# A transformer block on one core: one of four query weight sums made anew on VectorE, output products that advance two token tiles together, and smaller changes to what is loaded when

## Chip, core and metric

The kernel runs on one NeuronCore of one Trainium2 chip. The metric is the device time of one execution in microseconds (us), lower is better. The time before is the median of seven executions. In addition one execution was recorded by the hardware profiler; all stage times below are from that record.

## What is computed

One conditioned transformer block on 2048 tokens of width 1024, in bf16 (the reference, cut to what matters):

```
mod = silu(c) @ w_mod            # six rows of 1024: sa, ca, ga, sb, cb, gb
h = layernorm(x) * (1 + ca) + sa
q = h @ wq                       # 32 query heads of 128 -> wq is 1024 x 4096
k, v = last 512 rows of the caches, 4 kv heads, each used by 8 query heads
o = softmax(q k^T / sqrt(128)) v # per head, 2048 x 512 scores
x = x + ga * (o @ wo)            # wo is 4096 x 1024
h = layernorm(x) * (1 + cb) + sb
x = x + gb * ((silu(h @ w_gate) * (h @ w_up)) @ w_down)    # 3584 wide
```

## The kernel before

**Fast products.** The query projection (except for the first eight heads), the output projection (except in the first chunk) and the feed-forward part are done by a Strassen-Winograd scheme: a 2 x 2 block product takes seven block products in place of eight. It needs four sums of weight blocks and four sums of input blocks. `PRO` and `product` give the seven products: A11 B11, A12 B21, four of a sum S by a sum T (number 0 to 3 in the lists), one of S4 by B22, and one of A22 by the last T.

**Stages.** The tokens are worked in four chunks of 512. In chunk 0 (to about 197 us in the profile) attention runs over 32 heads, and the output projection is a plain one (`oproj_plain`). Chunks 1 to 3 each have 32 heads of attention (about 197 to 310, 360 to 468, 517 to 629 us) and then `oproj` (to about 360, 517 and 675 us). The feed-forward part follows, in two stretches of 1024 tokens.

**One iteration of attention.** The loop variable `i` counts heads over all chunks (`NA` = 128), `h` is the head within the chunk. In an iteration TensorE does, in this order: a part of the query projection for heads four ahead (`q_first` or `q_third`), the scores of head `i + 1`, another part (`q_second` or `q_fourth`), and the product with the values (`pv`) of head `i`. VectorE drains the query products (L636, L640, L674) and normalises the attention output (reciprocal L707, product L708). ScalarE does the exponentials (L691). The engines are in order; the tracker `T.op` sets the semaphore waits from the buffers that an instruction reads and writes.

**Query weights and their sums.** Four heads share one group of weights. Per group and chunk, `load_wq` (L301) loads the weights, into one of two slots. The four sums T of a group are formed on VectorE once, in chunk 0 (`weight_sums`, L579), into a slot of `tq`, and stored to a DRAM tensor `wq_sums` (`store_sums`, L590), 1024 KB per group. Chunks 1 to 3 load all four back (`load_sums`, L596). The load for the group two ahead is emitted at `i % 4 == 0`, and waits until TensorE has done the last product of the group two before it, since there are two slots. The sum with number 1 is used first in a group, by product 6 in `q_second`; sum 1 is b22 minus sum 0.

**The SP queue.** SyncE (SP) issues in order, and one queue carries in attention: the weight loads, the sums, the loads of `x` (L389 for the next layer norm, L275 for the residual, four per chunk at h = 8, 12, 16, 20), the columns of `w_mod` (L902), the transposes of each head's output (`oturn`, L714) and of the normalised input (`ln_turn`, L372), both by DMA, and ten of the output projection's weight units (`load_unit`, L806).

**The output projection's units.** Weights come in 28 units of 512 KB per chunk, four per product of `PRO`, in ten slots. In chunks 1 to 3 the first ten are loaded by SP at h = 5, 7, ... 23. Within `oproj` each of two token tiles (`k`) runs through a whole product before the other. A slot is free after the second tile is through it, so `load_unit(ch, u + NUN, 1)`, issued by ScalarE's queue, is emitted at 5/8, 6/8, 7/8 and 8/8 of each product. The partial results are copied from PSUM by ScalarE (L862, L864) or added into the residual on VectorE (`take_product`, L884 to L888).

**Second layer norm, and the sums of w_down.** `ln2[1]` normalises the second half of the first feed-forward stretch; it starts at h = 14 of chunk 3, and whatever is not done is finished at h = 29. `wd_sums` forms four sums of `w_down` in a single buffer `t_` during the first stretch, and stores them (L1331) with one DMA of 512 KB per row block, after the fourth sum.

Of the kernel before, what the change touches and what calls it, by code (L numbers as in the profile page):

```python
# [3 lines left out]
ALU = mybir.AluOpType  # L4
# [38 lines left out]
class _Tracker:  # L43
    def __init__(self):
        self.synced = {}

    def op(self, st, emit, reads=(), writes=(), after=()):


        req = {}  # L50

        def need(s, c):
            if req.get(s, 0) < c:
                req[s] = c

        for b in reads:
            if b.last_write is not None:
                need(*b.last_write)
        for b in list(writes) + list(after):
            if b.last_write is not None:  # L60
                need(*b.last_write)
            for s, c in b.reads.items():
                need(s, c)
        if st.dma and st.count:
            need(st, st.count)
        done = self.synced.setdefault(id(st.issuer), {})
        for s, c in req.items():
            if s is st and st.self_exempt:
                continue
            if done.get(s, 0) >= c:  # L70
                continue
            st.issuer.wait_ge(s.sem, c)
            done[s] = c
        ins = emit()
        st.count += st.inc
        ins.then_inc(st.sem, st.inc)
        for b in reads:
            b.reads[st] = st.count
        for b in writes:
            b.last_write = (st, st.count)  # L80
            b.reads = {}
# [37 lines left out]
def bass_adaLN_cond__sliding_block_cached__swiglu_ffn__prompt_kernel(  # L119
# [140 lines left out]
    with nc.Block() as block:  # L260

        @block.gpsimd
        def _(g):
# [281 lines left out]
            B_tq = [bufs("tq%d_" % i, 4) for i in range(NWQ)]  # L545
            tq = [M.take((AT_TQ + 8 * i) * KB, [4, 4, 256], F16, B_tq[i]) for i in range(NWQ)]
            Q_tq = [dq("q_tq%d" % i) for i in range(NWQ)]
            Q_ts = dq("q_ts")
            wq_t = nc.dram_tensor("wq_sums", (HG * 2, P, 4096), F16).ap()
            B_wqt = bufs("wqt", HG * 2)  # L550
# [30 lines left out]
            def weight_sums(g, st, e, which):  # L581
                sl = g % NWQ
                w_, t_, bt = wq_sb[sl], tq[sl], B_tq[sl]
                b11, b12, b21, b22 = w_[:, 0:4, 0:256], w_[:, 0:4, 256:512], w_[:, 4:8, 0:256], w_[:, 4:8, 256:512]
                for k in which:
                    x, y, extra = ((b12, b11, []), (b22, t_[:, 0], [bt[0]]), (b22, b12, []), (b21, t_[:, 1], [bt[1]]))[k]
                    tt_(st, e, t_[:, k], bt[k], x, y, ALU.subtract, B_wq[sl] + extra)

            def store_sums(g):
                T.op(Q_ts, lambda: SP.dma_start(wq_t[g % HG], tq[g % NWQ].rearrange("p a b c -> p (a b c)")),  # L590
                     reads=B_tq[g % NWQ], writes=[B_wqt[g % HG]])

            def load_sums(g):
                if g >= NCH * HG:
                    return
                T.op(Q_tq[g % NWQ], lambda: SP.dma_start(tq[g % NWQ].rearrange("p a b c -> p (a b c)"), wq_t[g % HG]),  # L596
                     reads=[B_wqt[g % HG]], writes=B_tq[g % NWQ])

# [8 lines left out]
            def product(p0, m):  # L607
# [8 lines left out]
                for kc in range(4):  # L616
                    if t_i is not None:
                        lhsT, lb = tq[sl][:, t_i, kc, w_lo:w_lo + P], B_tq[sl][t_i]
                    elif m == 1:
# [162 lines left out]

            PRO = (("A11", "B11"), ("A12", "B21"), ("S2", 1), ("S1", 0), ("S3", 2), ("S4", "B22"), ("A22", 3))
            NPO = Hq // 2
# [5 lines left out]

            def load_unit(ch, u, st=0):

# [12 lines left out]
                e = (SP, A)[st]  # L805
                T.op(Q_un[st][sl], lambda: e.dma_start(dst, src), reads=rd, writes=[B_un[sl]])  # L806

            def o_first(ch, k, p):
# [3 lines left out]
                   [B_oT[2 * p][0], B_un[sl]], PB[(QBK, XBK)[k]], loose=True)  # L812

            def oproj(ch, done_first, each):
                ab, cb = [QBK, XBK], [OBK, OBK + 1]
                B_e1, B_u1, B_u2 = bufs("e1_", NPO // 4), bufs("u1_", 2), bufs("u2_", 2)
# [21 lines left out]
                sums(3)  # L838
                for n, (a_, _) in enumerate(PRO):
                    for k in range(2):  # L840
                        b = (ab, cb)[n in (1, 4, 6)][k]
                        for p in range(NPO):
                            if n == 0:
                                if (k, p) not in done_first:
                                    o_first(ch, k, p)
                            else:
                                lo, hi = slice(k * P, (k + 1) * P), slice(256 + k * P, 256 + (k + 1) * P)
                                lhsT, lb = {
                                    "A12": (oT[:, 2 * p + 1, lo], B_oT[2 * p + 1][0]), "A22": (oT[:, 2 * p + 1, hi], B_oT[2 * p + 1][1]),
                                    "S1": (e1[:, p, lo], B_e1[p // 4]), "S2": (oT_s[:, 2 * p, lo], B_oT[2 * p][0]),  # L850
                                    "S3": (oT_s[:, 2 * p, hi], B_oT[2 * p][1]), "S4": (oT_s[:, 2 * p + 1, lo], B_oT[2 * p + 1][0])}[a_]
                                u = n * (NPO // NPU) + p // NPU
                                sl = (ch * UPC + u) % NUN
                                mm(bank(b), lhsT, unit[sl][:, p % NPU, :], p == 0 and n in (1, 4), p == NPO - 1, [lb, B_un[sl]],
                                   PB[b], loose=True)
                            if p % NPU == NPU - 1:
                                u = n * (NPO // NPU) + p // NPU
                                if k == 1 and u + NUN < UPC:
                                    load_unit(ch, u + NUN, 1)
                                each()  # L860
                        if n in (0, 3):
                            T.op(ACT, lambda: A.activation(u1[k], bank(b), AF.Copy), writes=PB[b] + [B_u1[k]])  # L862
                        elif n == 2:
                            T.op(ACT, lambda: A.activation(u2[k], bank(b), AF.Copy), writes=PB[b] + [B_u2[k]])  # L864
                        else:
                            half, hf = {1: (0, 0), 4: (1, 1), 5: (0, 1), 6: (1, 0)}[n]
                            u_ = None if n == 5 else (u2[k], B_u2[k]) if n == 6 else (u1[k], B_u1[k])
                            take_product(b, u_, x_sb[:, 2 * half + k, :], BX[2 * half + k], ga_bc, B_ga[hf], hf, k)
                            if n >= 5:
                                keep_rows(ch * TPC + 2 * half + k)  # L870
                    if n == 0:
# [130 lines left out]
            for i in range(NA):  # L1002
                ch, h = divmod(i, Hq)
                p0 = i - i % 2 + LEAD
                if ch == 0 and h in (13, 17, 22):
                    load_wo((13, 17, 22).index(h))
                if ch and h % 2 and 5 <= h < 5 + 2 * NUN:
                    load_unit(ch, h // 2 - 2)
                if ch and h in (8, 12, 16, 20):
                    load_x(ch * TPC + h // 4 - 2)  # L1010
                at_xl = [AT_XL + 2 * j for j in range(3)]
# [4 lines left out]
                if ch == NCH - 1 and h == 3:  # L1016
                    ln2[0] = ln_task(range(TPC), True, at_xl, (AT_N, AT_N + 2), scale=(g2, B_g2, sb, B_sb))
                    tasks.append(ln2[0])
                if ch == NCH - 1 and h == 14:
                    finish(mod_rest)  # L1020
# [26 lines left out]
                if p0 >= PLAIN:  # L1047
                    if i % 2 == 0:
                        q_second(p0)
                    else:  # L1050
                        q_fourth(p0)
                exps(i + 1, 2)
                if h == Hq - 5 and ch + 1 < NCH:
                    input_sums((ch + 1) % 2, (0, 1))
# [17 lines left out]
                g = i // 4 + 2  # L1072
                if i % 4 == 0 and i >= 8 and g - 2 * 0 >= HG + 2:
                    load_sums(g)
# [231 lines left out]
            wd_t = nc.dram_tensor("wd_sums", (4, P, NPR * 512), F16).ap()  # L1306
            B_wdt = bufs("wdt", NPR)
            Q_ds, Q_dk = [dq("q_ds%d" % i) for i in range(2)], dq("q_dk")

            def wd_sums():  # L1310
# [13 lines left out]
                for r in range(NPR):  # L1324
                    w_ = dr[r % 2]
                    b11, b12, b21, b22 = w_[:, 0, 0:512], w_[:, 0, 512:D], w_[:, 1, 0:512], w_[:, 1, 512:D]
                    for k in range(4):
                        x, y, extra = ((b12, b11, []), (b22, t_[:, 0], [B_ds[0]]), (b22, b12, []), (b21, t_[:, 1], [B_ds[1]]))[k]
                        tt_(DVE, V, t_[:, k], B_ds[k], x, y, ALU.subtract, [B_dr[r % 2]] + extra)
                        yield  # L1330
                    T.op(Q_dk, lambda: SP.dma_start(wd_t[:, :, r * 512:(r + 1) * 512].rearrange("k p n -> p k n"), t_),  # L1331
                         reads=B_ds, writes=[B_wdt[r]])
                    load(r + 2)
# [10 lines left out]
            def load_wd(n):  # L1344
# [6 lines left out]
                for j in range(2):  # L1351
                    if isinstance(which, int):
                        src = wd_t[which][:, j * hp * CH:(j + 1) * hp * CH]
                        dst = wd[i][:, j * hp:(j + 1) * hp, :].rearrange("p a b -> p (a b)")
                        rd = B_wdt
                    else:
# [110 lines left out]
```

## Time and profile before

| | |
|---|---|
| time, median of 7 | 1185.4 us (1184.01 to 1188.8) |
| profiled execution | 1187.78 us; its span 1186.0 us |
| granted TensorE clock, mean | 0.996 |
| TensorE (PE) busy | 1155.0 us, 97% |
| VectorE (DVE) busy | 809.3 us, 68% |
| ScalarE (ACT) busy | 498.1 us, 42% |
| DMA moved | 253.42 MB, 214 GB/s on average |
| chain that ended last | PE 89%, DMA 6%, DVE 3% |
| load of a group's four sums | 1024 KB, 22 times, 7.2 us to landing |
| `x` load | 256 KB, 28 times, 6.1 us to landing |

The rows are shares over the whole span, and stages differ: in attention DVE is busy for up to 90% of some stretches, in the output projection much less. "PE busy" is time in which the profile has a matmul in flight; the number of matmuls in a stretch tells whether they come at full pace. The DMA share in windows is a sum over packets, and it can exceed 1[...].

### The profile page before, as it was taken

Reading aid. Unit: us, or ns where it says so; the run is one execution under the profiler, and the core shown is the slowest. Engines: PE = TensorE matmul, PEld = TensorE weight load, DVE = VectorE, ACT = ScalarE, POOL = GpSimd, SP = SyncE. Lnnn points to the kernel's source line nnn. Section 1 sums busy time; section 2 is a strip of 40 time slices with the busy share of each in tenths; the row PEclk is TensorE's granted clock in tenths of the full one; section 3 lists DMA queues with packets and bytes.
Section 4 is the critical chain, followed back from the end, with each engine's and each line's share of the span. In section 5 each row is a group of like instructions: output and inputs, shape, how many; then the busy total and the mean of one; then the engine's idle time right before and its main releaser. Section 6 shows DMA issues by size and latency. Waiting matters only on the chain.

```text
span 1186.0 us, 20701 instructions
## 1 busy us (share of the span) xinstructions
PE 1155.0 (97%) x7838; PEld 665.7 (56%) x7838; DVE 809.3 (68%) x1792; ACT 498.1 (42%) x736; POOL 20.3 (2%) x41
## 2 busy tenths in 40 slices
PE   6999999999999999999899999999999999999998
PEld 4677645777647777468674444444444444444443
DVE  4888737876728877457677588888457777776214
ACT  4676502666306765147561144444210344444110
POOL 1000000000000000000000000000010000000000
PEclk9999999999999999999999999999999999999999
DMA  9999796999769997959979766564896232321733
GB/s 304 234 269 260 209 357 220 304 283 288 214 234 251 296 302 182 305 143 274 266 179 284 239 197 194 164 200 138 272 285 191 72 106 73 96 83 62 249 133 133
DMA packets 282627, 253.42 MB, mean 214 GB/s; under 512 B 109728, under 2 KB 244896, under 8 KB 278688
## 3 DMA queue, kind: packets, MB, share of 16 engines
q1 hardware_dynamic: 252656, 189.70, 59.7%
q10 hardware_dynamic: 29872, 62.40, 15.2%
q8 instruction: 62, 1.02, 0.4%
q14 instruction: 37, 0.30, 0.1%
HBM read 195.04 MB, written 32.51 MB: 192 GB/s over the span
## 4 chain that ended last, share of the span: by engine, by line
PE 89%; DMA 6%; DVE 3%; SPq 1%; issue 1%; ACT 0%; POOL 0%; DVEq 0%
PE ps L265 89%; DMA arena<-wq_sums 3%; DMA arena<-arena 1%; DMA arena<-in_w_mod_dram 1%; SPq L284 1%; DMA wd_sums<-arena 1%; DVE arena L708 1%; DVE arena L1187 0%; DVE arena L579 0%; DVE arena L412 0%; DVE arena L640 0%; ACT arena L932 0%; DVE arena L674 0%; DVE arena L707 0%; DVE arena L376 0%
## 5 line engine op out<-in xcount | busy, mean ns | idle before, releaser
L265 PE MATMUL ps<-arena 128*128 128x512 bf16 (+5 forms) x7789 | 1151.6, 310 | 22.8 <-DMA arena<-wq_sums 8.2
L265 PEld LDWEIGHTS ps<-arena 128*128 128x128 bf16 (+1 forms) x7789 | 662.4, 98 | 511.2 <-issue 12.8
L691 ACT ACTIVATE arena<-ps 128x1024 bf16<-128x1024 f32 x256 | 249.8, 1022 | 39.3 <-PE ps L265 36.4
L579 DVE TENSOR_TENSOR arena<-arena 128x512 f16<-128x512 bf16 (+2 forms) x488 | 208.4, 471 | 25.4 <-DMA wo_sums<-arena 11.5
L634 ACT ACTIVATE arena<-ps 128x256 f32<-128x256 f32 x134 | 51.3, 383 | 195.2 <-PE ps L265 194.4
L1175 DVE TENSOR_TENSOR arena<-ps,arena 128x512 f16<-128x512 f32 x112 | 77.2, 689 | 39.4 <-PE ps L265 37.3
L1168 ACT ACTIVATE arena<-ps 128x512 f32<-128x512 f32 x112 | 66.9, 597 | 73.6 <-PE ps L265 73.6
L708 DVE TENSOR_TENSOR arena<-ps,arena 128x512 bf16<-128x512 f32 x128 | 88.5, 692 | 4.9 <-DVE arena L707 0.5
L1197 ACT ACTIVATE ps<-ps 128x512 f32<-128x512 f32 x56 | 32.6, 582 | 127.1 <-PE ps L265 126.9
L640 DVE TENSOR_TENSOR arena<-ps,arena 128x256 bf16<-128x256 f32 x180 | 75.6, 420 | 12.0 <-PE ps L265 8.2
L884 DVE TENSOR_TENSOR arena<-ps,arena 128x512 f32<-128x512 f32 x34 | 23.4, 690 | 84.2 <-PE ps L265 84.1
L1187 DVE TENSOR_TENSOR arena<-ps,arena 128x512 bf16<-128x512 f32 x56 | 38.5, 688 | 29.3 <-ACT arena L1182 29.3
L707 DVE RECIPROCAL arena<-ps 128x4 f32<-128x4 f32 x128 | 23.1, 181 | 40.6 <-PE ps L265 39.6
L887 DVE TENSOR_TENSOR arena<-ps,arena 128x512 bf16<-128x512 f32 x22 | 15.2, 689 | 46.4 <-PE ps L265 46.4
L1182 ACT ACTIVATE arena<-ps 128x512 f16<-128x512 f32 x56 | 33.3, 594 | 31.6 <-PE ps L265 31.6
L412 DVE BATCH_NORM_STATS2 arena<-arena 128x6 f32<-128x512 bf16 x56 | 38.5, 687 | 6.4 <-DMA arena<-x_mid 6.2
L915 DVE SCALAR_TENSOR_TENSOR arena<-arena 128x512 f32<-128x512 bf16 x56 | 41.6, 743 | 0.1
L1182 ACT ACTIVATE arena<-arena 128x512 f16<-128x512 f16 x56 | 34.8, 622 | 4.9 <-DVE arena L1175 4.9
L835 DVE TENSOR_TENSOR arena<-arena 128x1024 f16<-128x1024 bf16 (+1 forms) x48 | 29.7, 685 | 7.2 <-DMA arena<-arena 7.2
L636 DVE COPY arena<-ps 128x256 f32<-128x256 f32 x46 | 19.4, 421 | 20.1 <-PE ps L265 19.8
L363 POOL TENSOR_TENSOR arena<-arena 128x1 f32<-128x1 f32 x30 | 17.8, 592 | 872.8 <-DVE arena L361 870.0
L674 DVE CAST arena<-ps 128x256 bf16<-128x256 f32 x60 | 25.2, 420 | 8.4 <-PE ps L265 7.0
(61 smaller groups left out, 208.7 us busy)
## 6 DMA issues: line engine op xcount, KB each, us to landing
arena<-wq_sums SPq DMA_DIRECT2D x22, 1024.0 KB, 7.2
arena<-in_A_wq_dram SPq DMA_DIRECT2D x42, 512.0 KB, 5.1
arena<-wo_sums ACTq DMA_DIRECT2D x42, 512.0 KB, 6.4
arena<-in_B_w_gate_dram SPq DMA_DIRECT2D x28, 512.0 KB, 4.2
arena<-in_B_w_up_dram SPq DMA_DIRECT2D x28, 512.0 KB, 5.2
arena<-wd_sums ACTq DMA_DIRECT2D x16, 896.0 KB, 6.9
arena<-in_A_wo_dram SPq DMA_DIRECT2D x24, 512.0 KB, 7.0
arena<-in_B_w_down_dram ACTq DMA_DIRECT2D x12, 896.0 KB, 6.9
```

The source lines that it names most:

```text
L265: T.op(PE, lambda: TE.matmul(out_ap, lhsT, rhs, start=start, stop=stop, skip_group_check=loose), reads=reads, writes=bb)
L412: T.op(DVE, lambda: V.bn_stats(st_sb[i][:, 6 * hf:6 * hf + 6], x_[:, 512 * hf:512 * hf + 512]), reads=[bx], writes=[B_st[i]])
L579: T.op(st, lambda: e.tensor_tensor(dst, x, y, op), reads=reads, writes=[dst_b])
L634: T.op(ACT, lambda: A.activation(sn[k], bank(QBK, 256), AF.Copy), writes=PB[QBK] + [B_sn[k]])
L640: T.op(DVE, lambda: V.tensor_tensor(dst, bank(XBK, 256, off), sn[k], ALU.add), reads=[B_sn[k]], writes=PB[XBK] + [B_q[i % NQ]])
L691: T.op(ACT, lambda: A.activation(ex[i % NEX][:, kt:kt + 2, :], bank(SCB[kt], 1024).rearrange("p (a b) -> p a b", a=2), AF.Exp, scale=att_s ...
L708: T.op(DVE, lambda: V.tensor_tensor(o_sb[i % NOS].rearrange("p (a b) -> p a b", a=TPC), num, rl_bc, ALU.mult), reads=[B_rl], writes=both + ...
L915: T.op(DVE, lambda: V.scalar_tensor_tensor(acc, ms[:, kc, :], sc[:, kc:kc + 1], acc, op0=ALU.mult, op1=ALU.add), reads=[B_ms, B_sc, B_acc] ...
L1168: T.op(ACT, lambda: A.activation(fn[m][i], bank(b), AF.Copy), writes=PB[b] + [B_fn[m][i]])
L1175: T.op(DVE, lambda: V.tensor_tensor(ring[c_], bank(b), fn[m][i], ALU.add), reads=[B_fn[m][i]], writes=PB[b] + [bs[c_]])
L1182: T.op(ACT, lambda: A.activation(sl_[c_], src, AF.Silu), reads=reads, writes=writes + [B_sl[c_]])
L1187: T.op(DVE, lambda: V.tensor_tensor(dst, u_[0], s_[0], ALU.mult), reads=[s_[1]] + [x for x in u_[1:]], writes=[db] + list(bb))
```

## The change

1. **Three of four query sums are stored and loaded.** `TQ_AT` places sum 1 last in the slot; `wq_sums` has 3072 columns instead of 4096 (768 KB per group). In chunks 1 to 3 sum 1 is formed by VectorE at `i % 4 == 3`, ahead of that head's reciprocal, from the loaded weights and the loaded sum 0.
2. **Both tiles together.** In `oproj` the first four products run two units on tile 0, the same two on tile 1, then the other two units; the last three products run tile by tile as before, with two units at a time set free. S3 comes before S1 in `PRO`, and goes to the other pair of banks.
3. **Units.** Chunks 1 and 2 preload eight units, chunk 3 ten (`AHEAD`). The remaining loads come from a list of free slots, none before the second half of the first product; those in the first product also wait for the last head's transpose (`behind`).
4. **`x` loads** go from h = 8, 12, 16, 20 to the first product of `oproj`, behind the last transposes on SP.
5. **`ln2[1]`** starts at h = 10 instead of 14.
6. **`wd_sums`** stores the sums two by two, each as soon as its pair is formed, in two DMAs of 256 KB.

The core of the diff:

```diff
+            TQ_AT = (0, 3, 1, 2)
-            wq_t = nc.dram_tensor("wq_sums", (HG * 2, P, 4096), F16).ap()
+            wq_t = nc.dram_tensor("wq_sums", (HG * 2, P, 3072), F16).ap()
...
+            def kept_sums(g):
+                return tq_[g % NWQ][:, 0:3].rearrange("p a b c -> p (a b c)"), [B_tq[g % NWQ][k] for k in (0, 2, 3)]
...
-            PRO = (("A11", "B11"), ("A12", "B21"), ("S2", 1), ("S1", 0), ("S3", 2), ("S4", "B22"), ("A22", 3))
+            PRO = (("A11", "B11"), ("A12", "B21"), ("S2", 1), ("S3", 2), ("S1", 0), ("S4", "B22"), ("A22", 3))
...
+            AHEAD = [0] + [8] * (NCH - 2) + [NUN]
...
+                for n in range(len(PRO)):
+                    both = n < 4
+                    for part in range(1 if both else 2):
+                        for ws in ((0, 1), (2, 3)):
+                            for k in (0, 1) if both else (part,):
+                                for w_ in ws:
+                                    for p in range(NPU * w_, NPU * w_ + NPU):
+                                        o_mm(n, k, p)
+                                    each()
+                            if both or part:
+                                free.extend(n * PPU + w_ + NUN for w_ in ws)
+                            if n or ws[0]:
+                                while free:
+                                    u = free.pop(0)
+                                    if u < UPC:
+                                        load_unit(ch, u, 1, B_oT[hd(Hq - 1)] if n == 0 else ())
+                            if n == 0 and ws[0]:
+                                for t in range(TPC):
+                                    load_x(ch * TPC + t)
+                        if not both:
+                            product_done(n, part)
+                    if both:
+                        product_done(n, 0)
+                        product_done(n, 1)
...
-                if ch and h % 2 and 5 <= h < 5 + 2 * NUN:
+                if ch and h % 2 and 5 <= h < 5 + 2 * AHEAD[ch]:
                     load_unit(ch, h // 2 - 2)
-                if ch and h in (8, 12, 16, 20):
-                    load_x(ch * TPC + h // 4 - 2)
...
-                if ch == NCH - 1 and h == 14:
+                if ch == NCH - 1 and h == 10:
...
                 exps(i + 1, 2)
+                g = (i + 5) // 4
+                if i % 4 == 3 and HG + 2 <= g < NCH * HG:
+                    weight_sums(g, DVE, V, (1,))
...
                         tt_(DVE, V, t_[:, k], B_ds[k], x, y, ALU.subtract, [B_dr[r % 2]] + extra)
+                        if k % 2:
+                            T.op(Q_dk[k // 2], lambda: SP.dma_start(
+                                wd_t[k - 1:k + 1, :, r * 512:(r + 1) * 512].rearrange("k p n -> p k n"), t_[:, k - 1:k + 1]),
+                                reads=B_ds[k - 1:k + 1], writes=[B_wdt[k // 2][r]])
                         yield
-                    T.op(Q_dk, lambda: SP.dma_start(wd_t[:, :, r * 512:(r + 1) * 512].rearrange("k p n -> p k n"), t_),
-                         reads=B_ds, writes=[B_wdt[r]])
```

## The prediction

> **What bounds the kernel now.** I read the engines' busy times first, then who waited for whom, then the chain of waits, then windows of the stages, and at last the SP queue in order of time. PE is busy for 97% of the span, so only what stops or slows PE counts. The longest list of waits on PE (columns: total us, times, longest):
>
> ```profile
> PE ps L265 <- DMA arena<-wq_sums: 8.2, 5, 3.7
> PE ps L265 <- DVE arena L1187: 1.0, 2, 0.5
> ```
>
> The chain of waits shows where (start, us, what):
>
> ```profile
> 244.63 6.98 DMA arena<-wq_sums
> ...
> 261.43 7.57 DMA arena<-wq_sums
> ...
> 421.41 5.98 DMA arena<-wq_sums
> ...
> 579.64 7.70 DMA arena<-wq_sums
> ...
> 594.78 8.41 DMA arena<-wq_sums
> ```
>
> All five are loads of the four query sums in attention. The windows of these stages (us, then PE, PEld, DVE, ACT, POOL busy with counts, PEclk, DMA share, GB/s):
>
> ```profile
> 200.00:244.00 44.00, 43.94 (x453) 34.68 (x451) 39.38 (x94) 30.41 (x40) 2.19 (x4) 1.00 1.17 299
> 244.00:276.00 32.00, 27.22 (x270) 21.48 (x269) 20.80 (x50) 17.96 (x23) 0.00 (x0) 0.95 1.15 286
> 420.00:433.00 13.00, 12.00 (x124) 9.26 (x123) 10.57 (x28) 8.29 (x11) 0.00 (x0) 1.00 1.12 337
> 579.00:606.00 27.00, 22.22 (x212) 17.44 (x211) 18.06 (x47) 14.27 (x19) 1.09 (x2) 0.94 1.16 281
> ```
>
> The first is a good stretch: 10.3 matmuls per us. The other three have 4.8, 1.0 and 4.8 us of idle PE, with the DMA engines full (share above 1.1). A granted clock of 0.95 over 32 us and 0.94 over 27 us costs 1.6 us each besides. The SP queue shows why the loads come late:
>
> ```profile
> 200.12 0.58 SPq L596 DMA_DIRECT2D arena<-wq_sums  x1
> ...
> 228.77 0.52 SPq L596 DMA_DIRECT2D arena<-wq_sums  x1
> ...
> 244.63 0.55 SPq L596 DMA_DIRECT2D arena<-wq_sums  x1
> ...
> 245.71 4.28 SPq L372 DMA_TRANSPOSE arena<-arena  x1
> 250.08 4.52 SPq L714 DMA_TRANSPOSE arena<-arena  x2
> ...
> 261.43 0.54 SPq L596 DMA_DIRECT2D arena<-wq_sums  x1
> ```
>
> One load per four heads; at full pace two heads take 6.60 us (reciprocals L707 at 279.72 and 286.32), so a group takes 13.2. The loads are 15.9 to 16.8 us apart: SP falls behind, since a transpose that takes 1.2 us to issue on a free machine takes 4 to 5 when the DMA engines are full.
>
> **How late is too late.** A load may start when the last product of the group two back is through, 0.4 us after pv of the head before. For the load at 244.63 that is 236.2 (reciprocal at 235.73). Its first use, product 6, stands 1.7 us behind the reciprocal at 249.06, at 250.8. Window 14.6 us, landing 7.0, so SP may be 7.6 us late; it was 8.4, and PE waited 0.9. The same for 261.43: 11.9 late, 2.1 of wait, after a wait of 1.7 in which DVE stood behind a late transpose (L376). For 579.64: 10.4 late, landing 7.7, wait 3.7.
>
> **What the waits cost in all**, from the reciprocals against 6.60 per pair: heads from 249.06 to 282.80 are eight, 33.7 - 26.4 = 7.3 us; 418.08 to 440.25 are six, 22.2 - 19.8 = 2.4; 581.98 to 611.82 are seven (odd step 3.51), 29.8 - 23.3 = 6.5. Together 16.2.
>
> **The change part by part.**
>
> **1. Sums and `x` loads, what is removed from SP and the DMA engines.** Until the load at 261.43 there go: 256 KB from each of the four sums before it (from 200.12 on), two `x` loads (226.4, 242.5), 1.5 MB. At 299 GB/s that is 5.0 us of lateness: 11.9 becomes 6.9. For 244.63: 1.0 MB, 3.5 us, 8.4 becomes 4.9. For 579.64: four sums and three `x` loads (542.7, 557.3, 575.8) go, one more `x_mid` load (of the earlier `ln2[1]`) comes before it, 1.5 MB at 263 to 281 GB/s, 5.5 us: 10.4 becomes 4.9. For 594.78, 12.4 late, the 3.7 of wait before it goes too.
> The new allowance: DVE forms sum 1 first, so the load must land 0.68 us plus a semaphore, 0.75, earlier. What is a load of 768 KB worth? Rows: 1024 KB land in 7.2 us, the 256 KB of an `x` load in 6.1; between them 6.8, 0.4 less. The Trainium skill (DMA: Bandwidth & Descriptors, Rules for kernel authors) speaks against smaller transfers, and asks for at least 1 MiB per DMA for full bandwidth; its section on the anatomy of one DMA has 2 us plus bytes/436e3, fitted for another issue path, an estimate of 4.4 for 1 MB and 3.8 for 768 KB. By that the large load would lose efficiency and gain 0.6. Here both durations are waiting in full engines, so I take the rows' 0.4. Allowance 14.6 - 0.75 - 6.8 = 7.0. Against 4.9, 6.9 and 4.9: the stalls go, the worst (261.43) just so. I take 85% of 7.3, 80% of 2.4 and 85% of 6.5: 6.2 + 1.9 + 5.5 = 13.6 us.
> The clock is part of this. The rows show 0.73, 0.50, 0.50, 0.56 in the microseconds after the wait of 2.1 us. The skill's TensorE: Matmul & The Clock Gate (Part 1) has the clock halve after an idle window of some 3.4 us; by it only the wait of 3.7 would have cost clock, 1.6 less in the sum. The row decides: both count.
>
> **2. The sum on DVE.** 22 instructions of 128x1024 at 0.684 us (L579 between 200 and 300 us), 15.0 us of DVE, one per four heads: 5% of a group's 13.2. DVE is at 39.38/44 = 90% in the first half of chunks 1 and 2, and comes to 95%; in chunk 3 it is near 77%. Each stands in front of a reciprocal; after pv of one head PE has 2.6 us of other work (four quarter products of the queries at 0.43 and the scores at 0.85) before the next pv needs the banks, and DVE needs 0.68 + 0.18 + 0.69 = 1.55, so one alone is hidden. Where `w_mod` and layer-norm pieces have already piled up it is not. The nearest row is chunk 0, where DVE makes one sum per head: 44 to 76 us has DVE 29.73 of 32 and 321 matmuls where 10.3 per us give 330, about 0.9 us lost in 32. For about 95 us of such stretches 0 to 3 us; I take 1.2. Behind the waiting sum stand the reciprocal, and with it pv's banks and the transpose on SP; it waits longer only if a load lands later than 12.3 us after its release (the cast L674 ahead of it ends about 0.5 before the reciprocal at 249.06).
>
> **3. `oproj`.** No matmul is added or removed. PE has no wait there now (48 matmuls per 10 us, 6.7 us a product). Units 8 and 9, in chunks 1 and 2, are no longer there at the start: ScalarE issues them when the last transpose has landed, 314.83 in chunk 1 (DVE's wait ends there), they land some 6.5 later (6.4 and 6.6 by their rows), 321.3, and the third product begins at 316.7 (PE's end of the first, ScalarE copies it at 317.14) + 6.7 = 323.4: 2.1 us to spare, with 1 MB of `x` and units 10 to 13 in flight beside them. Later units have two products (13.4 us) where they had 1.6 to 2.1; from the fifth product on 1.5 (10 us), still above 6.6. `x` is needed at the end of the second product. ScalarE stands in these issues before the first copies, but the banks are used again only one product later, and S3's turn on the other banks covers both copies. Cost 0 to 4 us (two chunks by 2 us of lateness), I take 0.4. The two unit loads that SP no longer issues in chunks 1 and 2 help only after h = 20, when the queue catches up by itself: nothing.
>
> **4. `ln2[1]` four heads earlier.** Now its last piece is forced at h = 29: two statistics of 0.7 and the rest keep DVE from 618.80 to 621.85, pv waits 0.4 (PE idle 622.3 to 622.72), the step is 3.79 where its neighbours have 2.1 to 2.6, and SP waits for the last row before its transposes. Gain 1.2. The final wait of 1.6 us for a transpose (629.07) stays: SP still issues four L372 there.
>
> **5. `wd_sums`.** A store after all four sums makes the next first sum wait, twice, behind it L1187, which frees a bank:
>
> ```profile
> 716.53 3.48 DMA wd_sums<-arena
> 720.01 0.03 issue
> 720.04 0.02 DVEq L72
> 720.06 0.04 issue
> 720.11 0.06 DVE arena L579
> 720.17 0.28 issue
> 720.45 1.03 DVE arena L1187 x2
> ```
>
> PE idle 0.52 and 0.44 there. Stored by pairs, each pair is out one or three pieces sooner. Gain 0.95. 14 more issues of 0.37 us on SP, which waits for DVE most of that time: nothing.
>
> **Sum.** 13.6 + 1.2 + 0.95 - 1.2 - 0.4 = 14.2 us off. From the profiled execution's 1187.8 that is 1173.6; from the median, 2.4 lower, 1171.2. What is removed are waits, some of which the faster runs may not have had, so I take 1173.
>
> **The rivals.**
> A. The backlog stays in part. If transposes rather than bytes hold SP, half of the lateness taken off is lost; then about half of the 13.6 remains, and DVE costs 2: 6.8 + 2.2 - 2.4 = 6.6, some 1180. For: the SP gaps are at transposes, and the worst load has no margin. Against: they take 1.2 us when the engines are not full.
> B. DVE becomes the gate, slower than before. If loads land as late as now, DVE itself stands still from the 12.3th us after release, with reciprocal and drains behind it; each of the five late groups then costs 0.75 more (3.8), the dense stretches the full 3, units 4 more, against 2.1 won: 8.7 more, about 1192 to 1194. It decides from a lateness of 7 us that is not reduced.
> C. Units arrive late in `oproj`: 2 us in two chunks with the stalls gone, about 1177, within my range.
> D. No change: gains and costs cancel, 1183 to 1188. That the sums are not made anew can be excluded, the program has the 22 extra instructions.
>
> **How the numbers follow.** Forecast with C 0.62, A 0.26, D 0.04, B 0.08. About 0.2% (2.4 us) is what a measurement of this kernel can tell from no change. Faster 0.62 + 0.26 = 0.88, same 0.04, slower 0.08. Low end: all 16.2 + 2.2 won at no cost, from 1187.8 and from the median, 1167 to 1169: 1167. High end: A with the upper DVE cost of 3, 1181.
>
> **What would show it.** Right: no PE wait on `wq_sums` above 1 us, PE busy above 31.5 in 244 to 276, clock 1.00 there, loads of sums 13 to 14 us apart, DVE busy up by about 15 us, the L1331 wait gone. Wrong: L579 in chunks 1 to 3 waiting on `wq_sums`, PE waiting on L707/L708 in the first halves of chunks 1 and 2, or on `wo_sums` at the third product.

## The result and the profile after

The changed kernel takes 1176.9 us (median of 12 runs, 1175.19 to 1180.3) against 1185.51 us before (31 runs); the ratio is 0.9925, 95% interval 0.9914 to 0.9935, some 8.9 us less (8.6 between the medians). The profiled execution took 1176.66 us, span 1174.7 us, against 1187.78 and 1186.0. The forecast was 1173.0, range 1167 to 1181, and faster.

Who waited for whom on PE in the changed kernel (total us, times, longest). Lines have moved: L580 is the old L579, L603 the load L596, L713/L714 the reciprocal and its product, L646 the old L640.

```profile
PE ps L265 <- DMA arena<-in_w_mod_dram: 5.0, 3, 4.3
PE ps L269 <- DVE arena L347: 3.6, 1, 3.6
PE ps L265 <- DVE arena L646: 1.8, 3, 0.6
```

The 8.2 us on `wq_sums` and the 1.0 us on L1187 are gone; the first two lines are the start of the kernel, where the earlier profile had the same time under another releaser (the first reciprocal of chunk 1 is at 199.01 us after, 199.07 before). What is new stands in the waits of VectorE:

```profile
DVE arena L580 <- DMA arena<-wq_sums: 2.2, 2, 1.9
```

The attention of chunk 1 in the windows view, before, after, and the run without the sum that is told below (columns as in the prediction: PE, PEld, DVE, ACT, POOL busy and counts, PEclk, DMA share, GB/s):

```profile
200.00:310.00 110.00, 105.16 (x1066) 83.14 (x1065) 86.75 (x203) 71.58 (x92) 2.19 (x4) 0.98 1.08 279
```

```profile
200.00:310.00 110.00, 107.89 (x1086) 83.67 (x1084) 93.04 (x215) 71.61 (x92) 2.19 (x4) 1.00 1.03 248
```

```profile
200.00:310.00 110.00, 109.02 (x1088) 85.66 (x1103) 91.89 (x213) 72.00 (x94) 2.20 (x4) 1.00 1.02 255
```

After the change PE has 2.7 us more work in the same window and the clock is whole, but VectorE has 6.3 us more, and PE is still idle for 2.1. Most of the 6.3 us is the work of heads that come sooner: without the sum VectorE still has 5.1 more than before, and PE is idle for 1.0. The loads of the sums on the SP queue of the changed kernel:

```profile
225.51 0.54 SPq L603 DMA_DIRECT2D arena<-wq_sums  x1
...
239.98 1.19 SPq L603 DMA_DIRECT2D arena<-wq_sums  x1
...
256.24 0.53 SPq L603 DMA_DIRECT2D arena<-wq_sums  x1
...
269.21 0.53 SPq L603 DMA_DIRECT2D arena<-wq_sums  x1
```

They are 3.3 to 5.5 us earlier than the loads of the kernel before at 228.77, 244.63, 261.43 and 274.71, and 14.5, 16.3 and 13.0 us apart. Counted from their release (0.4 us behind the reciprocals at 236.13 and 249.49) the second and third are 3.4 and 6.3 us late, where 4.9 and 6.9 were forecast. The last one here still comes too late for VectorE. First its line in the chain of waits (start, us to landing), then VectorE in order of time:

```profile
269.21 8.57 DMA arena<-wq_sums
```

```profile
275.59 0.43 DVE L680 CAST arena<-ps 128x256 bf16<-128x256 f32 x1
277.89 0.69 DVE L580 TENSOR_TENSOR arena<-arena 128x1024 f16<-128x1024 bf16 x1 [1.88 <-DMA arena<-wq_sums]
278.50 0.18 DVE L713 RECIPROCAL arena<-ps 128x4 f32<-128x4 f32 x1
```

The new sum waits 1.88 us for its load, and the reciprocal behind it waits with it: that step takes 5.08 us where the kernel without the sum takes 3.1; the next one is 0.6 shorter, 2.92 for 3.52. Fifteen microseconds later no load is late, and the sum still costs:

```profile
290.19 0.43 DVE L680 CAST arena<-ps 128x256 bf16<-128x256 f32 x1 [0.81 <-PE ps L265]
290.54 2.01 DVE L580 TENSOR_TENSOR arena<-arena 128x1024 f16<-128x1024 bf16 x3
292.46 0.18 DVE L713 RECIPROCAL arena<-ps 128x4 f32<-128x4 f32 x1
```

Three sums stand in a row there: the new one, and two of `input_sums` that h = 27 always has. The step is 4.44 us, before 3.84.

**Where the time came from, by stage**, from the first reciprocal of a chunk to its last, in the profiled executions. For chunk 1 these are the lines of VectorE before, after, and without the sum:

```profile
199.07 0.18 DVE L707 RECIPROCAL arena<-ps 128x4 f32<-128x4 f32 x1 [0.41 <-PE ps L265]
...
309.37 0.18 DVE L707 RECIPROCAL arena<-ps 128x4 f32<-128x4 f32 x1 [0.48 <-PE ps L265]
```

```profile
199.01 0.18 DVE L713 RECIPROCAL arena<-ps 128x4 f32<-128x4 f32 x1 [0.41 <-PE ps L265]
...
305.11 0.17 DVE L713 RECIPROCAL arena<-ps 128x4 f32<-128x4 f32 x1
```

```profile
200.29 0.18 DVE L713 RECIPROCAL arena<-ps 128x4 f32<-128x4 f32 x1 [0.41 <-PE ps L265]
...
303.74 0.18 DVE L713 RECIPROCAL arena<-ps 128x4 f32<-128x4 f32 x1 [0.48 <-PE ps L265]
```

| us | before | after | without the sum |
|---|---|---|---|
| chunk 1 | 110.30 | 106.10 | 103.45 |
| chunk 2 | 105.58 | 105.37 | 104.42 |
| chunk 3, with its last heads | 107.32 | 101.41 | 100.55 |
| projection, last reciprocal of chunk 1 to the first of chunk 2 | 51.86 | 51.83 | 51.86 |
| from the last reciprocal to the end of the span | 560.0 | 559.15 | 559.3 |

The gain lies in attention, but for some 0.9 us behind it, and nothing of it in the output projection.

### The profile page after: what moved, and what is told of

Same layout as the page of the kernel before. It is cut to its first block, busy times and chain, and to the rows that moved or that the text cites. A ratio compares the mean times of both kernels' runs of the same rounds, so it can differ in the third digit from the quotient of the medians.

```text
span 1174.7 us, 20785 instructions
## 1 busy us (share of the span) xinstructions
PE 1151.4 (98%) x7838; PEld 663.4 (56%) x7838; DVE 819.5 (70%) x1814; ACT 497.6 (42%) x736; POOL 20.5 (2%) x41
## 4 chain that ended last, share of the span: by engine, by line
PE 92%; DVE 3%; DMA 2%; SPq 1%; issue 1%; ACT 0%; DVEq 0%
PE ps L265 92%; DMA arena<-in_w_mod_dram 1%; SPq L284 1%; DMA arena<-wq_sums 1%; DVE arena L580 1%; DVE arena L714 1%; DVE arena L844 1%; DVE arena L376 0%; DVE arena L646 0%; DMA arena<-arena 0%; ACT arena L964 0%; DVE arena L680 0%; DVE arena L713 0%; DVE arena L947 0%; DVE arena L642 0%
## 5 line engine op out<-in xcount | busy, mean ns | idle before, releaser
L580 DVE TENSOR_TENSOR arena<-arena 128x512 f16<-128x512 bf16 (+3 forms) x510 | 223.2, 480 | 26.1 <-DMA arena<-in_A_wo_dram 16.2
L640 ACT ACTIVATE arena<-ps 128x256 f32<-128x256 f32 x134 | 51.4, 383 | 172.7 <-PE ps L265 172.0
L1201 ACT ACTIVATE arena<-ps 128x512 f32<-128x512 f32 x112 | 66.9, 597 | 73.5 <-PE ps L265 73.5
L714 DVE TENSOR_TENSOR arena<-ps,arena 128x512 bf16<-128x512 f32 x128 | 88.5, 691 | 4.9 <-DVE arena L713 0.5
L916 DVE TENSOR_TENSOR arena<-ps,arena 128x512 f32<-128x512 f32 x34 | 23.4, 689 | 87.3 <-PE ps L265 87.2
L646 DVE TENSOR_TENSOR arena<-ps,arena 128x256 bf16<-128x256 f32 x180 | 75.6, 420 | 10.7 <-PE ps L265 6.7
L713 DVE RECIPROCAL arena<-ps 128x4 f32<-128x4 f32 x128 | 23.0, 180 | 35.0 <-PE ps L265 34.5
L868 ACT ACTIVATE arena<-ps 128x512 f32<-128x512 f32 x12 | 6.8, 596 | 60.1 <-PE ps L265 60.1
```

What stands on the lines that cost most here:

```text
L580: T.op(st, lambda: e.tensor_tensor(dst, x, y, op), reads=reads, writes=[dst_b])
L640: T.op(ACT, lambda: A.activation(sn[k], bank(QBK, 256), AF.Copy), writes=PB[QBK] + [B_sn[k]])
L646: T.op(DVE, lambda: V.tensor_tensor(dst, bank(XBK, 256, off), sn[k], ALU.add), reads=[B_sn[k]], writes=PB[XBK] + [B_q[i % NQ]])
L714: T.op(DVE, lambda: V.tensor_tensor(o_sb[i % NOS].rearrange("p (a b) -> p a b", a=TPC), num, rl_bc, ALU.mult), reads=[B_rl], writes=both + ...
L1201: T.op(ACT, lambda: A.activation(fn[m][i], bank(b), AF.Copy), writes=PB[b] + [B_fn[m][i]])
```

## Experiments

All ratios are to the kernel before, measured beside the run, with 95% intervals. Theory 1: the lighter SP queue removes the waits, and the sum on VectorE gives some of it back. Theory 2: the sum is free, and what is missing is lateness that stayed. A rival for the projection: its steadier slots carry the gain.

### Relief and price of the sums, apart

`all_four`: four sums loaded, none made. `no_sum`: three loaded, none made. `four_and_sum`: four loaded, and the one made besides. The edits on the changed kernel (`...` marks lines that are left out):

```diff
 # all_four and four_and_sum
-wq_t = nc.dram_tensor("wq_sums", (HG * 2, P, 3072), F16).ap()
+wq_t = nc.dram_tensor("wq_sums", (HG * 2, P, 4096), F16).ap()
...
-return tq_[g % NWQ][:, 0:3].rearrange("p a b c -> p (a b c)"), [B_tq[g % NWQ][k] for k in (0, 2, 3)]
+return tq_[g % NWQ].rearrange("p a b c -> p (a b c)"), B_tq[g % NWQ]
 # all_four and no_sum
-                g = (i + 5) // 4
-                if i % 4 == 3 and HG + 2 <= g < NCH * HG:
-                    weight_sums(g, DVE, V, (1,))
```

> The changed kernel with all four query sums loaded, 1024 KB per group, and none made on VectorE; everything else of the change stays. Theory 1 (the lighter queue removes the waits, and the sum on VectorE gives a few us back): lateness is still cut by the x loads, but 256 KB per group come back; part of the waits on wq_sums returns, 2 to 5 us of PE waits, and some 3 us of VectorE's cost go, so 1176 to 1181. Theory 2 (VectorE's sum costs nothing, what remains is lateness): slower than the changed kernel by the returned waits alone, 1180 to 1184.

> The changed kernel with the 22 sums on VectorE left out: three sums are loaded, and product 6 of chunks 1 to 3 uses what lies in the fourth slot, so the values are not those of the reference. It is the change's relief without its price. Theory 1: 3 to 5 us faster than the changed kernel, 1172 to 1174, and the steps of 3.9 and 4.4 us at every fourth head go back to 3.5 and 3.8. Theory 2: within 1 us of the changed kernel, 1176 to 1178.

> The changed kernel with all four sums loaded and the one made on VectorE besides (the same value twice): the price without the relief. Theory 1: slower than the kernel with four loaded by 3 to 5 us, because each sum stands ahead of a reciprocal and waits for a late load, some 1182 to 1186. Theory 2: within 1 us of the kernel with four loaded.

| | median us | ratio | interval |
|---|---|---|---|
| changed kernel | 1176.9 | 0.9925 | 0.9914 to 0.9935 |
| all_four | 1177.27 | 0.9921 | 0.9899 to 0.9943 |
| no_sum | 1173.49 | 0.9885 | 0.9866 to 0.9904 |
| four_and_sum | 1182.27 | 0.9951 | 0.9931 to 0.9970 |

With three loaded, the sum costs 0.9925 - 0.9885 = 0.0040, 4.7 us (3.7 us by a repeat of the changed kernel, 0.9916, told below); with four loaded 0.9951 - 0.9921 = 0.0030, 3.6 us. The smaller loads bring 0.0036, 4.3 us, without the sum. In the last two comparisons the intervals overlap, so those sizes are rough. So relief and price cancel: the first part of the change, beside the other parts, moves nothing that can be measured. Theory 2 falls.

The profiles show where the two sides stand. `all_four` takes 107.33, 104.35 and 100.48 us for the three chunks, `no_sum` 103.45, 104.42 and 100.55. The smaller loads help in chunk 1 alone, by 3.9 us, while the sum has its price in all three chunks (2.65, 0.95 and 0.86 us in the table above). The only wait of PE for the sums in `all_four` lies in chunk 1:

```profile
PE ps L265 <- DMA arena<-wq_sums: 2.0, 1, 2.0
```

A kernel that makes the sum in chunk 1 only was not run. In the profile of `four_and_sum` VectorE waits for the loads, and PE for VectorE:

```profile
DVE arena L580 <- DMA arena<-wq_sums: 9.0, 6, 2.4
```

```profile
PE ps L265 <- DVE arena L646: 3.9, 7, 0.6
...
PE ps L265 <- DVE arena L580: 2.9, 3, 1.1
```

### The first part alone, on the kernel before

`before_sums` is the kernel before with three sums stored and loaded and the one made at `i % 4 == 3`, as the changed kernel does it, and nothing else.

> The kernel before with the first part alone: three sums loaded, one made on VectorE. Theory (relief and price nearly cancel beside the other parts, but alone the queue is later): three quarters of the load relief, 3 to 4 us of lateness off, against 3 to 5 us of VectorE's cost and waits of VectorE for late loads: 1182 to 1186, no clear gain. Rival (the smaller sums are the main gain): 1177 to 1179.

Measured 1184.47, ratio 0.9981, 0.9968 to 0.9994: a gain of some 2 us, at the edge of what can be told. Its profile (1188.29 us, 3.8 above its median) shows what became of the waits on the loads:

```profile
DVE arena L580 <- DMA arena<-wq_sums: 11.7, 5, 3.1
```

```profile
PE ps L265 <- DVE arena L580: 5.3, 4, 1.8
```

The loads come at 241.12, 258.40 and 271.36, too late for VectorE, which holds the reciprocal back. This is what rival B of the prediction describes, but its price was too high: the kernel is not slower than before. That the smaller loads' own relief makes up for it fits the 4.3 us above; a kernel before with three loaded and none made was not run.

### The x loads

`x_back` puts the four `x` loads back to h = 8, 12, 16, 20 in the changed kernel; `before_x` moves them into the projection in the kernel before, and does nothing else. In the kernel before, an `x` load stands close ahead of each of the late loads of sums on SP, with one transpose between:

```profile
242.46 0.80 SPq L275 DMA_DIRECT2D arena<-in_A_x_dram  x1
...
259.23 0.83 SPq L275 DMA_DIRECT2D arena<-in_A_x_dram  x1
```

```diff
 # before_x
-                if ch and h in (8, 12, 16, 20):
-                    load_x(ch * TPC + h // 4 - 2)
 ...
                     if n == 0:
+                        for t in range(TPC):
+                            load_x(ch * TPC + t)
                         sums(2)
```

> The changed kernel with the x loads back in attention (h = 8, 12, 16, 20). Theory (the lighter queue is what removes the waits): lateness of the sums rises by some 0.8 us per x load, 256 KB at about 299 GB/s, up to 2.5 us, and waits on wq_sums return behind VectorE's sum: 1 to 4 us slower than the changed kernel, 1178 to 1181. If only the smaller sums matter, no change, 1176 to 1178.

> The kernel before with the x loads moved to the output projection alone. Theory (these loads stand in the late stretch of the queue and cost nothing elsewhere): the waits on wq_sums fall by half or more, 1179 to 1182. Rival (x loads are too small to matter): 1184 to 1186.

`x_back`: 1180.28, ratio 0.9949 (0.9932 to 0.9965). `before_x`: 1179.43, ratio 0.9934 (0.9919 to 0.9950). So the moved `x` loads alone bring 0.0066, some 7.8 us, where the first part alone brings some 2. The repeat of the changed kernel beside them (0.9916) is 2.1 us faster, with intervals that overlap: all other parts together add no more than that. Putting the `x` loads back into the changed kernel loses 2.8 us (3.9 by the repeat). In `x_back` the loads of the sums come later again by 2.1 to 2.4 us:

```profile
242.08 1.23 SPq L603 DMA_DIRECT2D arena<-wq_sums  x1
...
258.66 0.53 SPq L603 DMA_DIRECT2D arena<-wq_sums  x1
...
271.46 0.53 SPq L603 DMA_DIRECT2D arena<-wq_sums  x1
```

The parts don't add: `x` loads and smaller sums both shorten the same lateness, and where a load comes in time, coming earlier brings nothing more (chunks 2 and 3 of `all_four`). In the profile of `before_x` PE waits in two places for `wq_sums`, in the kernel before in five (8.2 us):

```profile
PE ps L265 <- DMA arena<-wq_sums: 2.5, 2, 2.0
```

Whether the bytes of the `x` loads count, or their place on SP, was not separated.

### The projection in the old order

`oproj_old` is the changed kernel with the old `oproj`, the old order of S1 and S3, and ten units loaded ahead in each chunk; the `x` loads stay in the projection.

```diff
-            AHEAD = [0] + [8] * (NCH - 2) + [NUN]
+            AHEAD = [0] + [NUN] * (NCH - 1)
...
-                for n in range(len(PRO)):
-                    both = n < 4
+                for n, (a_, _) in enumerate(PRO):
+                    for k in range(2):
 ...
```

> The changed kernel with the output projection in the old order (one token tile after the other, S1 before S3), ten units loaded ahead in all three chunks; the x loads stay in the projection. Theory: in the projection nothing stood on PE's path before or after (51.86 and 51.83 us from the last reciprocal of chunk 1 to the first of chunk 2), so only the two further unit loads in chunks 1 and 2 count, after h = 20: within 1 us of the changed kernel. Rival (the steadier slots are where the gain is): 3 us or more slower, with PE waiting on wo_sums.

Measured 1175.18, ratio 0.9904 (0.9886 to 0.9922): not slower, nominally 2.5 us faster than the changed kernel, with intervals that overlap. The rival falls. It had been expected within 1 us of the changed kernel. In the profiles 1.6 of the 2.6 us between the two kernels lie in attention of chunk 1, ahead of the first projection that differs: the load at h = 20 is not late there, and its step takes 3.11 us instead of 5.08. The order of the projection cannot do that; why it was in time stays open. The stretch from chunk 1 to chunk 2 is 51.83 us, as with the new order. The new order seems to have a small price in chunk 3: from the last reciprocal to the end the old order takes 558.6 us, the new one 559.15 and, in the repeat, 560.5. This is PE there in a repeat of the changed kernel (`after_again`):

```profile
632.95 15.77 PE L265 MATMUL ps<-arena 128*128 128x512 f16 x71 [0.31 <-DVE arena L916]
648.99 1.02 PE L265 MATMUL ps<-arena 128*128 128x512 bf16 x4 [0.26 <-DMA arena<-in_A_wo_dram]
651.28 13.97 PE L265 MATMUL ps<-arena 128*128 128x512 bf16 x63 [1.27 <-DMA arena<-in_A_wo_dram]
```

Both tiles' sums now leave the second pair of banks together, on a VectorE that is full in this stretch (the wait on L916), and units for the sixth product come 1.5 us late. In the first profile of the changed kernel only the wait on L916, 0.28, is there; `all_four`, `mixed` and `ln2_wd_old` show 0.6, 1.0 and 1.5 us on `in_A_wo`, `oproj_old` none; `no_sum` and `x_back`, which have the new order too, show none either.

### The layer norm and the w_down sums

`ln2_wd_old` undoes both small parts in the changed kernel.

```diff
-                if ch == NCH - 1 and h == 10:
+                if ch == NCH - 1 and h == 14:
 ...
-                        if k % 2:
-                            T.op(Q_dk[k // 2], lambda: SP.dma_start( ...
+                    T.op(Q_dk[0], lambda: SP.dma_start(wd_t[:, :, r * 512:(r + 1) * 512].rearrange("k p n -> p k n"), t_),
```

> The changed kernel with the second layer norm at h = 14 again and the w_down sums stored by one DMA. Theory: 1.2 us at the end of chunk 3 and 0.95 us in the first feed-forward stretch come back, about 2 us slower than the changed kernel; the waits are seen at the last heads of chunk 3 and at two places with L1220. Rival: x_mid loads that are later are out of the crowded stretch, and the sums of chunk 3 land earlier: no change or faster.

Measured 1178.98, ratio 0.9933 (0.9916 to 0.9950), nominally 1 to 2 us slower, intervals overlapping. The traces are plainer than the times. PE in the last heads, and PE's waits:

```profile
614.64 1.95 PE L265 MATMUL ps<-arena 128*128 128x129 bf16 x20 [0.43 <-DVE arena L714]
```

```profile
PE ps L265 <- DVE arena L1220: 1.0, 2, 0.5
```

Both waits in the first stretch are back, and so is the step of 3.79 us (2.63 in the changed kernel). But the step behind it is back too, and that one was shorter: 2.08 us for 2.63. These are the reciprocals at h = 28, 29 and 30 before, and after:

```profile
617.97 0.18 DVE L707 RECIPROCAL arena<-ps 128x4 f32<-128x4 f32 x1 [1.83 <-PE ps L265]
...
621.76 0.17 DVE L707 RECIPROCAL arena<-ps 128x4 f32<-128x4 f32 x1
...
623.84 0.18 DVE L707 RECIPROCAL arena<-ps 128x4 f32<-128x4 f32 x1 [1.17 <-PE ps L265]
```

```profile
608.13 0.18 DVE L713 RECIPROCAL arena<-ps 128x4 f32<-128x4 f32 x1 [1.83 <-PE ps L265]
...
610.76 0.18 DVE L713 RECIPROCAL arena<-ps 128x4 f32<-128x4 f32 x1 [1.72 <-PE ps L265]
...
613.39 0.18 DVE L713 RECIPROCAL arena<-ps 128x4 f32<-128x4 f32 x1 [1.72 <-PE ps L265]
```

So the last heads gain 0.6 us by the earlier layer norm, not 1.16. It has a price besides: even without the sum the steps from h = 14 to 15 and from 20 to 22 are together 0.3 us longer than before, and some 0.3 us are left.

### Other places for the sum

`sum_behind` moves the sum behind the reciprocal and its product. `pool_sum` gives it to GpSimd. `mixed` stores all four and makes the one only for the groups loaded at h = 8, 12, 16, where SP is late.

```diff
 # pool_sum
-                    weight_sums(g, DVE, V, (1,))
+                    weight_sums(g, POOL, G, (1,))
 # mixed
+            def made(g):
+                return g >= HG + 2 and 4 * (g - 2) % Hq in (8, 12, 16)
...
-                if i % 4 == 3 and HG + 2 <= g < NCH * HG:
+                if i % 4 == 3 and g < NCH * HG and made(g):
...
```

> The changed kernel with the sum on VectorE issued behind the reciprocal and the product of its head instead of ahead of them. Theory 1 (place of the sum): the late load at the seventh group no longer holds the reciprocal back, and the 0.4 us steps at group starts shrink; 1 to 2.5 us faster, 1174 to 1176. If the sum's mere 0.68 us of VectorE is the price, no change, 1176 to 1178; and if it now comes too late for product 6, PE waits on L580 and it is slower by 1 to 2 us.

> The changed kernel with the 22 sums on GpSimd, which is busy for 2% of the span, in place of VectorE. Theory (VectorE's 0.68 us ahead of each fourth reciprocal costs 3 to 4 us): most of the price goes, 1173 to 1175, near the kernel without the sum. If the sum takes much longer there (over 3 us), product 6 waits for it at every group, 22 times 1 us or more: 1190 and above; and if VectorE is slowed while GpSimd runs, something between.

> The changed kernel with all four sums stored, and all four loaded except for the groups loaded at h = 8, 12 and 16 of chunks 1 to 3, where three are loaded and the one is made on VectorE at h = 11, 15, 19 (9 sums instead of 22). Theory (the sum costs where VectorE is full or has the input sums beside it, h = 3, 7, 27, and pays only where SP is late, in the middle of a chunk): most of the 3.4 us between the changed kernel and the one without the sum come back, 1173 to 1175. If the relief is needed in the early groups too, waits on wq_sums come back at h = 15 to 20, 1177 to 1179.

> The changed kernel as it is, beside the three others on the same chip: ratio to the kernel before 0.991 to 0.994.

| | median us | ratio | interval |
|---|---|---|---|
| sum_behind | 1178.13 | 0.9932 | 0.9910 to 0.9955 |
| pool_sum | 1183.16 | 0.9977 | 0.9964 to 0.9991 |
| mixed | 1175.00 | 0.9910 | 0.9894 to 0.9925 |
| after_again | 1176.55 | 0.9916 | 0.9903 to 0.9929 |

Behind the reciprocal the sum costs as much as ahead of it, 1.64 + 1.55 + 1.27 = 4.5 us in the three chunks of the profile. The 1 to 2.5 us that were expected of the place did not come: no late load is seen, but the steps behind it grow (4.12 where the kernel without the sum has 3.5, twice), and PE waits for the sum:

```profile
PE ps L265 <- DVE arena L580: 2.3, 3, 1.1
```

The place only moves the price; what both places share is 0.68 us more work for a VectorE that is full there.

On GpSimd it is worse. The groups of `pool_sum` (the first over the span, the second in 200 to 300 us), and the second group in the changed kernel:

```profile
L580 POOL TENSOR_TENSOR arena<-arena 128x1024 f16<-128x1024 bf16 x22 | 47.2, 2143 | 354.2 <-PE ps L265 354.2
```

```profile
L947 DVE SCALAR_TENSOR_TENSOR arena<-arena 128x512 f32<-128x512 bf16 x20 | 19.6, 978 | 0.0
```

```profile
L947 DVE SCALAR_TENSOR_TENSOR arena<-arena 128x512 f32<-128x512 bf16 x21 | 15.6, 742 | 0.0
```

The sum takes some 2.14 us there (spans on GpSimd are rough in a profile), three times as long, and the `w_mod` products on VectorE take 978 ns on average instead of 742. The profiled execution took 1196.4 us, 13 above the median, and other waits differ in it too, so only these durations are read from it; how the 6 us of loss divide is not shown.

Beside `oproj_old`, `mixed` has the shortest profile of the kernels that leave nothing out: 104.74, 104.27 and 100.98 us for the three chunks, where the changed kernel has 106.10, 105.37 and 101.41. By the timed runs (0.9910 against 0.9916) the two can't be told apart. No version that clearly beats the changed kernel was found.

## Why the prediction was right, and which term was off

- **Bound and place: right.** PE, stopped in attention by late loads of the sums. The waits of 8.2 us on `wq_sums` are gone, the clock stays at 1.00 in 200 to 310 us, and the loads come 3 to 5.5 us earlier.
- **Step 1, the relief, 13.6 us: right in size, not in its parts.** Without the sum's price the chunks gain 110.30 - 103.45 = 6.9, 105.58 - 104.42 = 1.2, and 107.32 - 100.55 = 6.8, of which 6.5 stand in the two steps that had waited for loads (8.80 and 4.77 us before, 3.5 each without the sum): together 14.6 (forecast 6.2, 1.9, 5.5). Of the 16.2 us of waits, 1.2 in chunk 2 were none: a step of 4.66 us at h = 21 was counted in, and it stands there in the kernel without the sum too. The rest fell almost whole, where 80 to 85% had been taken. The bytes were counted too low: the `x` loads at 242.46 and 259.23, close ahead of the loads at 244.63 and 261.43, were left out, and 1.5 MB was taken as 1.5 million bytes. The prediction booked `x` loads and sums together; `before_x` shows that the `x` loads alone bring some 7.8 us.
- **Step 2, the sum on VectorE, 1.2 us: the mis-sized term.** It costs 2.65 + 0.95 + 0.86 = 4.5 us in the profiles (4.0 in the repeat) and 3.7 to 4.7 by the ratios, above the whole range of 0 to 3 that was given. The scaling from chunk 0 saw only the dense first halves, and these cost 0.4 us a chunk. Three other things were left out or put at nothing: h = 27, where two input sums stand beside it (0.6 us in each of chunks 1 and 2); chunk 3, called near 77% full, where pieces of two layer norm tasks now stand beside the sum (0.9 us; with the second task started later, in `ln2_wd_old`, the step from h = 14 falls from 3.84 to 3.11); and the late load that holds up VectorE, and with it the reciprocal (1.6 us in chunk 1, 1.1 in the repeat).
- **The allowance of 7.0 us** at 269.21 was just missed: that load landed in 8.57 us where 6.8 had been taken. What cost the time was the other limit, which the prediction named and priced at nothing: VectorE stands still from the 12.3th us after the release, and this load landed 13.9 us after it (0.4 behind the reciprocal at 263.45).
- **Why SP is late: not as told.** In the profile before, long transposes did stand where the DMA engines were full (4.28 us at 245.71, share 1.12). But at 239.60 and 243.35 a transpose took 1.19 us to issue, at shares of 1.28 and 1.16: a full DMA does not by itself make it long, and what does is not shown.
- **Step 3, the projection, 0.4 us:** right that no gain lies there. The spare time of units 8 and 9 in chunks 1 and 2 was enough; the small waits came in chunk 3, which had been put at nothing, at other units and at L916, 0.3 to 1.8 us.
- **Step 4, the layer norm, 1.2 us: too high.** The step of 3.79 us fell by 1.16, but the next one grew by 0.55, which had not been counted; some 0.3 us are left.
- **Step 5, 0.95 us: right,** 0.85 from the last reciprocal to the end.
- **The sum:** 14.2 forecast, 11.1 in the profiled executions. Step 2 took 3.3 more and step 4 brought 0.9 less, while the relief brought 1.0 more. Between medians the gain is 8.6, because the profiled execution of before was 2.3 us above its median; the prediction had taken a middle value for this.
- **Signs.** Those of being right came, but for two: the loads are 14.5, 16.3 and 13.0 us apart, not 13 to 14, and VectorE's busy time rose by 10.2 us, not 15 (809.3 to 819.5). One sign of being wrong came, L580 waiting on `wq_sums` in chunk 1, and it marks the term that was off.
- **Rivals:** A did not come about; the lateness fell by 5.0 and 5.6 us where the two loads were forecast to gain 3.5 and 5.0. C's number, 1177, is the one that was measured, but by chance: its cause, units late in chunks 1 and 2, did not occur. B's mechanism was seen, in `before_sums`, but it did not turn the sign.

## What to carry to other kernels

Look first at what stands in an in-order issue queue ahead of the transfer that is late, and can wait for another stage: moving four loads of 256 KB per chunk brought 7.8 us alone and cost nothing elsewhere, where a quarter off the late transfer, paid for with a sum on another engine, brought some 2. When a transfer is traded for work on another engine, cost the work where that engine is fullest and where its neighbours pile up, head by head, not by its mean share; make the trade only in the stage where the transfer is still late, here chunk 1 (a kernel that does so was not run); and note that an engine which waits for the transfer in order holds back all that stands behind it. Gains that draw on the same lateness do not add: on top of the moved loads, the other five parts together brought some 2 us.

## What the runs showed of the hardware that was not expected

The same subtraction of 128x1024 takes 0.684 us on VectorE and some 2.14 us on GpSimd, and with it on GpSimd the `scalar_tensor_tensor` products on VectorE went from 742 to 978 ns on average, while the drains from PSUM (L646, 419 ns; L714, 691 ns) kept theirs. A load of 768 KB landed in 6.0 us in the median, against 7.2 for 1024 KB before. Most of that is the lighter traffic: with four sums loaded in the otherwise changed kernel (`all_four`) 1024 KB landed in 6.5 us, so the size alone is worth some 0.5, near the 0.4 that was taken. A single load of 768 KB still took 8.57.
